# Two large groups' slices run in pairs, one scattering for both small groups, and a reordered front in an attention and mixture-of-experts kernel

## The chip, the cores and the metric

The kernel runs on one core of a Trainium2 chip. The metric is the device time in microseconds (us); less is better. The core's engines run side by side, each through its own queue in order: PE (TensorE) does matmuls and transposes and writes only to PSUM, DVE (VectorE) and ACT (ScalarE) do elementwise work and read PSUM, POOL (GpSimd) does elementwise work on SBUF, and SP issues DMA transfers.

## The reference

Three stages, in float32. First a linear attention, in four batches of 576 tokens, eight heads of 64:

```python
q_s = softmax(q, over the head dimension);  k_s = softmax(k, over the tokens)
kv  = einsum('bhsd,bhse->bhde', k_s, v)
x   = einsum('bhsd,bhde->bhse', q_s, kv)          # laid out as (2304, 512)
```

Then a mixture of experts: each token goes to the one of eight experts with the largest logit of `x @ w_gate`, up to a capacity of 576 tokens for each expert, and the output is `gate * (relu(x @ w1[e]) @ w2[e])`, with w1 512 x 1024 and w2 1024 x 512. The last stage is a second mixture with its own weights, added to its input, and only for tokens with `x @ w_skip > 0`.

## The kernel before

x lies transposed in SBUF: 128 partitions by 4 chunks of features by 576 tokens. A batch's attention is done in two halves of four heads: a and b are batch 0, c and d batch 1, e and f batch 2, g and i batch 3.

Nearly all tokens of a batch go to one expert. The kernel guesses that expert from the attention (`guess`), loads its weights, and runs all 576 tokens through it as a *large group*; the few tokens of another expert (at most 32) are gathered, put through it as a *small group* and scattered back. There are five large groups, in this order: first mixture for batches 0, 1 and 2, called (0, 0), (0, 1) and (0, 2), then second mixture for batches 0 and 1. Two small-group objects stand beside them: S (one small group, batch 2 of the first mixture) and T (two small groups, t = 0 and 1, batch 2 of the second mixture).

Each large group has 16 *slices*. Slices 0 to 7 make 128 features of the hidden layer each: 24 matmuls of 128x128 by 128x288 (`products`), because float32 is split into a high and a low part (`split`: ACT casts, DVE subtracts) and high-high, high-low and low-high are summed. `evacuate(s)` of these slices takes the result out of PSUM: ACT writes `hh` (relu, L876), then DVE writes `hl` (L877). Slices 8 to 15 make the output, two slices for each chunk, and the odd ones end with a DVE multiply by the gate into x. The slices use two PSUM pairs in turn (`banks`), so slice s can start once `evacuate(s-2)` has read its pair. `split_w(s)` makes a slice's weights `wh` (ACT) and `wl` (DVE) and runs two slices ahead; `L4` to `L7` are the loads of the group's later weights, `N0` to `N3` those of the next group's first, and `X0` to `X3` split the next group's x.

Between the slices stand the *words* of the table COURSE, one line for each slice, written by hand. Words left of the bar are issued between a slice's products and its evacuation, words right of it behind the evacuation. Since every engine goes through its queue in order, a line sets who stands behind whom. The words of an attention half (c.qm, c.km, ...): `qm` (DVE: maximum of q and its negative), `km`, `kt`, `kc` (maximum of k over the tokens: DVE, PE transposes with a DVE reduction, a PE matmul `pmax` and a DVE subtraction, L404), `ke` (ACT exponential of k, L411), `q1`, `q2`, `q3` (ACT: 7, 7 and 6 exponentials of q with sums, L334), `qn` (DVE normalization of q, L362 to L367), `kv` (PE and DVE), `qt` (PE transposes, ACT copies), `re` (PE, ACT copies into x). The words C1.g and C1.1 to C1.6 are the guess and the routing of batch 1; C1.5 is some 17 small DVE instructions, C1.6 some more with one ACT exponential between them. `G.0` and `G.3` make the gate.

Short PSUM results (`pl`, `pt`, `pmax`, `ptq`, `pts`, ...) share three banks in turn (`bank`, pool `pa` with `bufs=3`): the fourth waits until the first has been read.

The *front*, before group (0, 0), is straight code: a's and b's attention, with `warm_up(n)` putting n matmuls of no use in between. `first_products` runs slices 0 and 1 of the first group in halves of two chunks each, as chunks of x come ready.

A scattering (`put(t, i)`) of a small group multiplies the expert's output `y2` with a one-hot matrix `pT[t]` built by `places` and `place` (words v and a), in 8 matmuls (L1255), and adds the result to x in four DVE adds (L1259); i = 0, 1 stand for two chunks each.

Of the kernel before, what the change touches and what calls it, by code (L numbers as in the profile page):

```python
# [17 lines left out]
P = 128  # L18
# [22 lines left out]

COURSE = (
    ((0, 0), """
    L4 c.qm | C0.1 c.km
    c.q1 | c.kt
    L5 c.q2 | C0.2 c.kc
    C0.3 c.ke d.qm |
    L6 C0.4 c.q3 | c.kv  # L50
    C0.5 c.qn d.q1 |
    L7 d.km | c.qt d.kt
    C0.6 d.q2 | d.kc
    d.ke | c.re G.0
    d.q3 X0 | d.kv
    d.qn X1 e.ld |
    | d.qt
    | d.re C1.g N0
    X2 N1 | C1.1
    X3 N2 | C1.2  # L60
    C1.3 e.qm N3 f.ld | C1.4
    """),
    ((0, 1), """
    L4 C1.5 |
    e.km e.q1 | e.kt
    L5 C1.6 e.q2 | G.3 e.kc
    e.ke f.qm | G.1
    L6 e.q3 | e.kv
    e.qn f.q1 | G.2
    L7 f.km | e.qt f.kt  # L70
    f.q2 | f.kc
    f.ke | e.re
    f.q3 X0 | f.kv
    f.qn X1 |
    | f.qt
    | f.re C2.g N0
    X2 N1 | C2.1
    X3 N2 | C2.2
    C2.3 N3 g.ld | C2.4
    """),  # L80
    ((0, 2), """
    L4 C2.5 | M0.1
# [11 lines left out]
    N2 g.qn S.v0 | S.t03  # L94
    X2 | S.a0 g.qt
    N3 | S.t04
    X3 | S.u00 S.u01
    """),
    ((1, 0), """
    L4 G.3 | g.rw  # L100
    g.rx | M2.1
    L5 | M2.2 M1.1
    M2.3 | M2.4
# [14 lines left out]
    L4 G.3 | T.t03 O0.2  # L118
    | T.a0 i.rw
    L5 i.rx | T.t04 C3.1  # L120
    T.v1 | T.t10 T.u00
    L6 | T.u01 C3.2 G.1
    C3.3 | T.t11 C3.4 O0.3
    L7 C3.5 G.2 | T.t12 T.a1
    | T.t13
    Z B |
    | T.t14
    | T.u10
    | T.u11 O1.0
    | O2.0  # L130
    | O1.1 O2.1
    | O2.2
# [6 lines left out]
def kernel(  # L139
# [647 lines left out]
    class Group:  # L787
        def __init__(self, m, x, r, lo, last=False):
            self.m, self.x, self.r, self.lo, self.last = m, x, r, lo, last
            self.hs = []  # L790

        def load(self, i, half=None):
            if i < 4:
# [36 lines left out]
        early = []  # L830

        def products(self, s):
            if s < len(self.early):
                self.pt = self.early[s]
                return
            wh, wl = whs[s % NB], wls[s % NB]
            if s < NF:
                self.pt = banks()
                for a in range(2):
                    for c in range(NC):  # L840
                        for n, (u, w) in enumerate(((wh, xh), (wh, xl), (wl, xh))):
# [28 lines left out]

        def evacuate(self, s):
            if s < NF:
                hh = hp.tile([P, S], F32R, name="hh", tag="hh", bufs=NF)
                hl = hp.tile([P, S], F32R, name="hl", tag="hl", bufs=NF)
                src = self.pt[:, :, :HT]
# [11 lines left out]
            else:  # L887
                return
            y = halves(self.x[:, c])[:, w]
            src, gate = self.pt[:, w, :HT], halves(self.mg)[:, w]  # L890
# [37 lines left out]

        def gate(self):

            self.gate_weights()
# [18 lines left out]
    with tc.tile_pool(name="fp", bufs=1) as fp:  # L950
# [58 lines left out]
        def q_norm(h, hs):  # L1009
            h.inverse(hs)  # L1010
            h.norm(hs)

        def q_turn(h, c):
            pt = bank("ptq")
# [31 lines left out]
        warm_up(2)  # L1046
        k_sub(b)
        k_v(a)
        warm_up(16)
        v_ones(b)  # L1050
        k_exp(b)
        a.qm()
        a.exp_sub(H01, ALLJ)
        a.exps([(2, j) for j in range(NJ)])
        a.exp_act(H01, ALLJ)
        k_v(b)
        k_v_norm(a)
        b.qm()
        a.exps([(3, j) for j in range(NJ)])
        warm_up(12)  # L1060
        b.exp_sub(H01, ALLJ)
        k_v_norm(b)
        b.exps([(2, j) for j in range(NJ)])
        b.exp_act(H01, ALLJ)
        b.exps([(3, j) for j in range(NJ)])
        a.sum_bulk(H01, ALLJ)
        RT["C0"].guess()
        first.eid = load_reg(gid[0], [ET.SP], 7)
        first.load(0, 0)
# [43 lines left out]
    hp = ctx.enter_context(tc.tile_pool(name="hp", bufs=1, reuse_waits="tile"))  # L1113
# [8 lines left out]
    class Small:  # L1122
# [69 lines left out]
        def expert(self, t, step):  # L1192
# [4 lines left out]
            if step != 2:  # L1197
                for i in {0: (0, 1), 1: (2, 3), 3: (4, 5), 4: (6, 7)}[step]:
                    w = self.tw.pop(8 * t + i)
                    for g in range(4):  # L1200
                        if i < 4:
                            lhsT, rhs = self.xs[:, i, 32 * t:32 * t + 32], w[:, 256 * g:256 * g + 256]
                        else:
                            lhsT = self.hT[:, g % 2, 32 * (i - 4):32 * (i - 4) + 32]
                            rhs = w.rearrange("p (u d) -> p u d", u=2)[:, g % 2, 256 * (g // 2):256 * (g // 2) + 256]
                        nc.tensor.matmul(  # L1206
                            out=self.ph[32 * g:32 * g + 32, :256], lhsT=lhsT, rhs=rhs, start=(i % 4 == 0), stop=(i % 4 == 3)
                        )
                    self.load(8 * t + i + 3)
            if step == 1:  # L1210
# [7 lines left out]
                nc.vector.tensor_copy(out=self.hT, in_=pt[:, :2 * P].rearrange("p (u s) -> p u s", u=2))  # L1218
            elif step == 4:
                for i in range(2):  # L1220
                    sl, cs = slice(64 * i, 64 * i + 64), slice(2 * i, 2 * i + 2)
                    src = self.ph[sl, :256].rearrange("p (c d) -> p c d", c=2)
                    nc.scalar.copy(y2[0][sl, cs], src)
                    nc.vector.tensor_sub(y2[1][sl, cs], src, y2[0][sl, cs].bitcast(F32))

        def places(self, t):
            cs = hp.tile([P, TINY], F32, name="cs2", tag="cs2")
            nc.vector.tensor_scalar(out=cs, in0=iota, scalar1=self.r["tlo"][:, t:t + 1], scalar2=None, op0=ALU.add)
# [18 lines left out]
            nc.tensor.transpose(pt[:, 0:LAST], p4f[:LAST, 4], ident[:LAST, :LAST])  # L1247
            nc.scalar.copy(pT[:, 4 * P:S], pt[:, 0:LAST])

        def put(self, t, i):  # L1250
            for c in (2 * i, 2 * i + 1):
                for a in range(2):
                    pt = bank("pts")
                    for n, u in enumerate(y2):
                        nc.tensor.matmul(  # L1255
                            out=pt[:, :HT], lhsT=u[:, c], rhs=self.pT[t][:, tokens(a)], start=(n == 0), stop=(n == 1)
                        )
                    x = self.x[:, c, tokens(a)]
                    nc.vector.tensor_add(x, x, pt[:, :HT])  # L1259
# [83 lines left out]
    for kk, (_, plan) in enumerate(COURSE):  # L1343
        lines = plan.strip().split("\n")
        assert len(lines) == NS
        for i, line in enumerate(lines):
            before, _, after = line.partition("|")
            groups[kk].products(i)
            n = NS * kk + i + 2
            if n < NS * len(COURSE):  # L1350
                groups[n // NS].split_w(n % NS)
            for w in before.split():
                word(kk, w)
            if n < NS * len(COURSE) + 1:
# [16 lines left out]
    def all_groups(s):  # L1371
# [9 lines left out]
        with tc.If(n >= 1):  # L1381
            with tc.For_i(0, n, 1):
# [98 lines left out]
```

## Time and profile before

| | |
|---|---|
| median of 3 runs | 416.97 us (416.24 to 419.02) |
| the profiled execution | 416.55 us, of which the span of instructions 414.7 us |
| PE busy | 393.7 us, 95% of the span |
| DVE busy | 251.6 us, 61% |
| ACT busy | 182.3 us, 44% |
| POOL busy | 12.4 us, 3% |
| mean granted TensorE clock | 0.995 |

Busy times are of one profiled execution, and a busy PE isn't PE at its peak, as matmuls are pipelined. What an engine waits for is told by the profile's releasers. The group (0, 0) runs from about 45 to 113.8 us of the span, (0, 1) from 113.8 to 182.9 us.

### The profile page before, as it was taken

The numbers are of one execution on the slowest core, as the hardware profiler recorded it, in microseconds if no ns is written. First come the engines' busy times: TensorE is split into PE (matmuls) and PEld (weight loads), VectorE is DVE, ScalarE is ACT, GpSimd is POOL, SyncE is SP. The second block draws the span as 40 slices with busy tenths as digits, with TensorE's granted clock in tenths as the row PEclk, the third lists the DMA queues.
The fourth block names the chain that finished last, engine by engine and source line by source line (L and its number), as shares of the span: only waits on it lengthen the run. The fifth ranks groups of instructions, "written<-read, shape, count | busy, mean of one in ns | idle before, by whom it ended". The sixth has DMA issues, their size and how long they took to land.

```text
span 414.7 us, 8456 instructions
## 1 busy us (share of the span) xinstructions
PE 393.7 (95%) x3241; PEld 351.1 (85%) x3241; DVE 251.6 (61%) x640; ACT 182.3 (44%) x547; POOL 12.4 (3%) x46
## 2 busy tenths in 40 slices
PE   8989898999999999999999999999999999899892
PEld 4656797898999989799999888899998988799881
DVE  4874789463586846278546656367777736654432
ACT  1656675734357772324346622333375342331211
POOL 2400000000000000000000100000000000000000
PEclk9999999999999999999999999999999999999998
DMA  8829926100970400293355771116315556363133
GB/s 207 220 54 262 255 72 193 31 2 2 295 182 9 124 2 2 82 300 96 107 195 178 217 216 52 51 52 232 101 53 183 182 180 214 92 204 123 31 101 102
DMA packets 72535, 54.48 MB, mean 131 GB/s; under 512 B 18454, under 2 KB 67114, under 8 KB 72490
## 3 DMA queue, kind: packets, MB, share of 16 engines
q1 hardware_dynamic: 70536, 53.60, 44.4%
q10 hardware_dynamic: 1954, 0.31, 0.6%
q8 instruction: 26, 0.43, 0.4%
q14 instruction: 19, 0.16, 0.1%
HBM read 49.16 MB, written 4.73 MB: 130 GB/s over the span
## 4 chain that ended last, share of the span: by engine, by line
PE 85%; DVE 8%; ACT 3%; issue 2%; DVEq 0%; ACTq 0%
PE pair L863 31%; PE pair L842 25%; PE pair L535 3%; PE px L495 3%; PE pxs L1150 2%; PE pk L437 2%; PE pl L596 2%; PE pto L1284 2%; PE ph L1206 1%; PE py L1206 1%; PE pts L1255 1%; PE pk L992 1%; PE ptq L463 1%; DVE hl L877 1%; PE pair L822 1%
## 5 line engine op out<-in xcount | busy, mean ns | idle before, releaser
L863 PE MATMUL pair<-hh,wh 128*128 128x288 f32 x320 | 98.3, 307 | 0.0
L863 PE MATMUL pair<-hh,wl 128*128 128x288 f32 x320 | 94.6, 296 | 0.0
L863 PE MATMUL pair<-hl,wh 128*128 128x288 f32 x320 | 94.5, 295 | 0.0
L842 PE MATMUL pair<-xh,wh 128*128 128x288 f32 x304 | 92.8, 305 | 0.0
L842 PE MATMUL pair<-xl,wh 128*128 128x288 f32 x304 | 89.6, 295 | 0.0
L842 PE MATMUL pair<-xh,wl 128*128 128x288 f32 x304 | 89.5, 295 | 0.0
L785 DVE TENSOR_TENSOR wl<-ws,wh 128x512 fp32r<-128x512 f32 x80 | 54.9, 686 | 35.9 <-ACT wh L784 35.4
L863 PEld LDWEIGHTS pair<-hh,wh 128*128 128x128 f32 x320 | 60.5, 189 | 3.8 <-issue 2.6
L863 PEld LDWEIGHTS pair<-hl,wh 128*128 128x128 f32 x320 | 60.7, 190 | 0.1
L876 ACT ACTIVATE hh<-pair 128x576 fp32r<-128x576 f32 x40 | 25.8, 645 | 79.2 <-PE pair L842 77.4
L863 PEld LDWEIGHTS pair<-hh,wl 128*128 128x128 f32 x320 | 60.5, 189 | 0.0
L842 PEld LDWEIGHTS pair<-xh,wh 128*128 128x128 f32 x304 | 57.1, 188 | 2.2 <-issue 0.9
L842 PEld LDWEIGHTS pair<-xl,wh 128*128 128x128 f32 x304 | 57.2, 188 | 0.1
L842 PEld LDWEIGHTS pair<-xh,wl 128*128 128x128 f32 x304 | 57.1, 188 | 0.0
L877 DVE SCALAR_TENSOR_TENSOR hl<-pair,hh 128x576 fp32r<-128x576 f32 x40 | 30.2, 755 | 37.1 <-ACT hh L876 37.1
L784 ACT CAST wh<-ws 128x512 fp32r<-128x512 f32 x80 | 49.3, 620 | 2.2 <-DMA ws<-in_moe_w_dram 1.5
L334 ACT ACTIVATE eq<-qt,mx 128x64 f32<-128x64 f32 x140 | 46.7, 338 | 0.5 <-DVE mx L323 0.5
L334 ACT ACTIVATION_READ_ACCUMULATOR eq<-qt,mx 128x1 f32 x140 | 26.6, 190 | 0.0
L535 PE MATMUL pair<-warm 128*128 128x384 f16 x94 | 18.7, 346 | 1.6 <-DVE warm L952 1.6
L785 DVE TENSOR_TENSOR xl<-x,xh 128x576 fp32r<-128x576 f32 x20 | 14.9, 752 | 6.0 <-ACT xh L784 6.0
L1285 ACT COPY ot<-pto 128x256 f32<-128x256 f32 (+1 forms) x24 | 7.0, 315 | 26.0 <-PE pto L1284 26.0
L535 PEld LDWEIGHTS <-warm 128*128 128x128 f16 x94 | 9.3, 104 | 8.1 <-issue 2.1
(210 smaller groups left out, 500.2 us busy)
## 6 DMA issues: line engine op xcount, KB each, us to landing
ws<-in_moe_w_dram SPq DMA_DIRECT2D x39, 512.0 KB, 4.7
tw<-in_moe_w_dram SPq DMA_DIRECT2D x24, 512.0 KB, 4.6
kt<-in_k_dram SPq DMA_DIRECT2D x8, 512.0 KB, 7.5
qt<-in_q_dram SPq DMA_DIRECT2D x8, 512.0 KB, 6.5
out_dram<-ot SPq DMA_DIRECT2D x12, 256.0 KB, 2.7
vt<-in_v_dram SPq DMA_DIRECT2D x16, 128.0 KB, 4.8
vt<-in_v_dram SPq DMA_DIRECT2D x3, 512.0 KB
mg<-gate SPq DMA_DIRECT2D x4, 288.0 KB, 7.2
```

Of the source, the lines that this page charges most:

```text
L334: nc.scalar.activation(self.eqv[:, h, j], self.qt[:, h, j], AF.Exp, bias=self.mx[:, i:i + 1], accum_out=self.qz[:, i:i + 1])
L437: nc.tensor.matmul(out=pk[64 * g:64 * g + 64, c * D1 + o:c * D1 + o + n], lhsT=self.kt[:rows(j), 2 * c + g, j], rhs=ones32[:rows(j), 0:1] ...
L495: nc.tensor.matmul(out=pt, lhsT=self.kd[:, c], rhs=self.qT[:, c, 0:4 * P], start=True, stop=True)
L535: nc.tensor.matmul(out=pw[:, 0, :3 * P], lhsT=warm16[:, 0:P], rhs=warm16, start=True, stop=True)
L596: nc.tensor.matmul(out=pl[32 * c:32 * c + 32, :HT], lhsT=self.weights[:, c], rhs=self.chunk(c, tokens(a)), start=True, stop=True,)
L784: nc.scalar.copy(hi, src)
L785: nc.vector.tensor_tensor(out=lo, in0=src, in1=hi.bitcast(F32), op=ALU.subtract)
L842: nc.tensor.matmul(out=self.pt[:, a, :HT], lhsT=u[:, c], rhs=w[:, c, tokens(a)], start=(c == 0 and n == 0), stop=(c == NC - 1 and n == 2),)
L863: nc.tensor.matmul(out=self.pt[:, a, :HT], lhsT=p_[:, f], rhs=w[:, tokens(a)], start=(v == 0 and f == 0 and n == 0), stop=(v == 1 and f == ...
L876: nc.scalar.activation(halves(hh), src, AF.Relu)
L877: nc.vector.scalar_tensor_tensor(out=halves(hl), in0=src, scalar=0.0, in1=halves(hh).bitcast(F32), op0=ALU.max, op1=ALU.subtract,)
L1150: nc.tensor.matmul(out=self.px[:, c * self.w:(c + 1) * self.w], lhsT=self.xt[:rows(j), c * P:(c + 1) * P], rhs=self.pj[:rows(j), j], start ...
```

## The change

Four edits:

1. *Pairs.* A line of COURSE may be `=`: its slice has no words, and its evacuation is issued behind the next slice's products. Slices 0 to 11 of (0, 0) and of (0, 1) are put in six such pairs each, with the words of both lines behind the second one's products, and some words moved by a line or more (c.km and d.km, e.km, C1.g, N0 and N1, f.ld). Slices keep their results in `pts`, by number.
2. *Shared scattering.* For the second small group, the halves of `y2` are written to the other partitions, and `places` builds one matrix that holds both groups; `put(i)` scatters both at once. T's four scatterings become two, behind the last of its words t; S's two stay, the second in the next group's first line.
3. *Front.* The subtraction of the maximum from half of q goes from DVE (`exp_sub`) to POOL (`q_sub`), warm-ups are cut from 94 matmuls to 74, q's normalization is split between other steps, and both halves' way to x stands ahead of `first_products`, which now has no other work between its halves than splits.
4. `gate_weights` is no longer called in `gate`, but by the word G.3, or by its own call in the general code.

```diff
-    L4 c.qm | C0.1 c.km
-    c.q1 | c.kt
-    L5 c.q2 | C0.2 c.kc
-    C0.3 c.ke d.qm |
-    L6 C0.4 c.q3 | c.kv
-    C0.5 c.qn d.q1 |
-    L7 d.km | c.qt d.kt
-    C0.6 d.q2 | d.kc
-    d.ke | c.re G.0
-    d.q3 X0 | d.kv
-    d.qn X1 e.ld |
-    | d.qt
-    | d.re C1.g N0
-    X2 N1 | C1.1
-    X3 N2 | C1.2
-    C1.3 e.qm N3 f.ld | C1.4
+    =
+    L4 c.qm c.km | C0.1 c.q1 c.kt d.qm
+    =
+    L5 c.kc | c.ke C0.2 c.q2 c.q3 d.km
+    =
+    L6 C0.3 c.qn | c.kv d.kt d.q1 d.q2
+    =
+    L7 C0.4 d.kc | c.qt d.ke C0.5 C0.6 d.q3 G.3
+    =
+    G.0 d.qn | d.kv c.re e.ld
+    =
+    C1.g X0 N0 N1 | d.qt X1
+    N2 | d.re f.ld
+    X2 N3 | C1.1
+    X3 | C1.2
+    C1.3 e.qm e.km | C1.4
...
-    L4 C1.5 |
-    e.km e.q1 | e.kt
-    L5 C1.6 e.q2 | G.3 e.kc
-    e.ke f.qm | G.1
-    L6 e.q3 | e.kv
-    e.qn f.q1 | G.2
-    L7 f.km | e.qt f.kt
-    f.q2 | f.kc
-    f.ke | e.re
-    f.q3 X0 | f.kv
-    f.qn X1 |
-    | f.qt
-    | f.re C2.g N0
+    =
+    L4 C1.5 | C1.6 G.3 e.q1 e.kt
+    =
+    L5 e.kc | G.1 e.ke e.q2 e.q3 f.km
+    =
+    L6 f.qm e.qn | e.kv f.kt f.q1 f.q2
+    =
+    L7 G.2 f.kc | e.qt f.ke f.q3
+    =
+    f.qn | e.re f.kv
+    =
+    C2.g X0 N0 N1 | f.qt X1
+    N2 | f.re
...
-    X3 | S.u00 S.u01
+    X3 | S.u0
...
-    L4 G.3 | g.rw
+    L4 G.3 | S.u1 g.rw
...
-    T.v1 | T.t10 T.u00
-    L6 | T.u01 C3.2 G.1
+    T.v1 | T.t10
+    L6 | C3.2 G.1
...
-    | T.u10
-    | T.u11 O1.0
+    | T.u0
+    | T.u1 O1.0
...
+            self.run(s)
+            self.pts[s] = self.pt
+
+        def run(self, s):
...
+        def q_sub(h):
+            nc.gpsimd.tensor_tensor(
+                out=h.eqv[:, H01], in0=h.qt[:, H01], in1=h.spread_q(h.mx, H01, ALLJ), op=ALU.add
+            )
...
         a.qm()
-        a.exp_sub(H01, ALLJ)
+        q_sub(a)
+        warm_up(4)
+        k_v(b)
...
-        a.sum_bulk(H01, ALLJ)
+        q_norm(a, H01)
         RT["C0"].guess()
...
-        q_norm(a, H01)
-        q_norm(a, H23)
-        warm_up(8)
+        warm_up(2)
         a.turn_new()
         q_turn(a, 0)
-        warm_up(3)
+        q_norm(a, H23)
+        warm_up(4)
         q_turn(a, 1)
...
+        b.turn_new()
+        q_turn(b, 0)
         x_main(a, 1)
         x_last(a)
-        first.split_x(0)
-        first.split_x(1)
-        first.split_w(0)
         warm_up(2)
-        b.turn_new()
-        q_turn(b, 0)
-        warm_up(3)
         q_turn(b, 1)
         q_last(b)
-        first.first_products(0, range(0, 2))
-        first.split_w(1)
+        first.split_x(0)
         x_main(b, 0)
+        first.split_x(1)
+        warm_up(2)
         x_main(b, 1)
         x_last(b)
-        first.first_products(1, range(0, 2))
+        first.split_w(0)
+        warm_up(4)
+        first.first_products(0, range(0, 2))
         first.split_x(2)
         first.split_x(3)
+        first.split_w(1)
+        first.first_products(1, range(0, 2))
         first.first_products(0, range(2, 4))
         first.first_products(1, range(2, 4))
...
+                        o = 32 * (g ^ 2 if t and i >= 4 else g)
...
-                    in1=cs.unsqueeze(1).to_broadcast(bb),
+                    in1=cs[:, (g // 2) ^ t if self.n == 2 else 0].unsqueeze(1).to_broadcast(bb),
...
-        def put(self, t, i):
+        def put(self, i):
+            pT = self.pT[i if self.n == 2 else 0]
...
             groups[kk].products(i)
+            if i and lines[i - 1].strip() == "=":
+                groups[kk].evacuate(i - 1)
             n = NS * kk + i + 2
             if n < NS * len(COURSE):
                 groups[n // NS].split_w(n % NS)
+            if line.strip() == "=":
+                continue
```

## Rows read from the trace of the kernel before

**Rows 1.** Busy time by stage: stretch, its length, each engine's busy time (instructions), clock, DMA.

```profile
45.10:113.80 68.70, 65.17 (x565) 59.17 (x563) 43.42 (x111) 38.11 (x128) 1.46 (x6) 1.00 0.42 113
113.80:182.90 69.10, 67.65 (x565) 62.73 (x564) 43.02 (x105) 37.46 (x125) 1.17 (x4) 1.00 0.33 91
```

**Rows 2.** Timeline of the front: start, duration, engine, line, operation, count [idle before].

```profile
15.19 1.76 POOL L985 COPY va<-vt 128x256 f32<-128x256 f32 x5 [2.29 <-DMA vt<-in_v_dram]
...
19.36 2.98 PE L992 MATMUL pk<-va,kt 128*128 128x130 f32 x20
...
26.62 0.14 DVE L587 TENSOR_SCALAR gid<-gid 1x1 int32<-1x1 int32 x1
...
30.11 1.12 PE L495 MATMUL px<-qT,kvd 128*128 128x512 f32 x2
...
31.55 0.82 DVE L367 TENSOR_TENSOR eq<-eq,qz 128x640 f32<-128x640 f32 x1
...
44.95 0.29 PE L822 MATMUL pair<-xh,wl 128*128 128x288 f32 x1
...
47.06 0.39 PE L842 MATMUL pair<-xh,wh 128*128 128x288 f32 x1
```

**Rows 3.** Timeline of DVE in the second large group.

```profile
115.08 0.19 DVE L688 TENSOR_TENSOR keep<-pos,rem 128x40 f32<-128x40 f32 x1
...
117.98 0.76 DVE L877 SCALAR_TENSOR_TENSOR hl<-pair,hh 128x576 fp32r<-128x576 f32 x1 [0.26 <-ACT hh L876]
118.65 0.68 DVE L785 TENSOR_TENSOR wl<-ws,wh 128x512 fp32r<-128x512 f32 x1
119.25 0.69 DVE L378 TENSOR_TENSOR m<-kt 128x512 f32<-128x512 f32 x1
...
127.88 1.48 DVE L404 TENSOR_TENSOR kt<-kt,pmax 128x1280 f32<-128x1280 f32 x1
...
129.88 1.48 DVE L320 TENSOR_REDUCE mx<-qt 128x20 f32<-128x1280 f32 x1
...
137.15 1.49 DVE L367 TENSOR_TENSOR eq<-eq,qz 128x1280 f32<-128x1280 f32 x1
```

**Rows 4.** Timeline of PE in the first large group: a word's transposes.

```profile
71.13 0.41 PE L386 MATMUL pt<-c,m 128*128 128x128 f32 x2 [1.64 <-DVE m L380]
```

**Rows 5.** Timeline of ACT in the second large group: the exponential of k.

```profile
129.46 1.28 ACT L411 ACTIVATE kt<-kt 128x1280 f32<-128x1280 f32 x1 [2.22 <-DVE kt L404]
```

**Rows 6.** The chain that ended last, both large groups: start, us, what ran.

```profile
47.33 2.33 ACT eq L334 x14
...
121.06 0.41 PE pt L386 x2
...
145.78 3.18 PE pair L863 x24
```

**Rows 7.** The same chain at the scatterings of S (two pieces) and T.

```profile
250.16 3.39 PE pair L863 x24
...
256.79 3.18 PE pair L842 x24
...
347.99 0.99 PE pts L1255 x6
...
349.54 3.19 PE pair L842 x24
...
355.13 0.49 PE ptl L608 x4
```

**Rows 8.** Busy time by stage at the span's end, columns as in rows 1.

```profile
408.00:408.50 0.50, 0.49 (x3) 0.25 (x3) 0.00 (x0) 0.19 (x1) 0.00 (x0) 1.00 0.84 218
...
410.50:411.00 0.50, 0.00 (x0) 0.00 (x0) 0.00 (x0) 0.00 (x0) 0.00 (x0) 0.70 0.94 268
```

**Rows 9.** Busy time of the warm-up line alone at the start: PE, weight loads, clock, DMA.

```profile
1.55:4.75 3.20, 3.20 (x11) 1.59 (x12) 1.00 0.82 224
4.75:7.00 2.25, 2.25 (x16) 1.36 (x14) 1.00 1.19 275
```

More of the change, by code (lines that the diff above doesn't have):

```diff
@@ L45 @@
     ((0, 0), """
-    L4 c.qm | C0.1 c.km
-    c.q1 | c.kt
-    L5 c.q2 | C0.2 c.kc
-    C0.3 c.ke d.qm |
-    L6 C0.4 c.q3 | c.kv
-    C0.5 c.qn d.q1 |
-    L7 d.km | c.qt d.kt
-    C0.6 d.q2 | d.kc
-    d.ke | c.re G.0
-    d.q3 X0 | d.kv
-    d.qn X1 e.ld |
-    | d.qt
-    | d.re C1.g N0
-    X2 N1 | C1.1
-    X3 N2 | C1.2
-    C1.3 e.qm N3 f.ld | C1.4
+    =
[14 more added lines that the diff above has]
+    C1.3 e.qm e.km | C1.4
     """),
     ((0, 1), """
-    L4 C1.5 |
-    e.km e.q1 | e.kt
-    L5 C1.6 e.q2 | G.3 e.kc
-    e.ke f.qm | G.1
-    L6 e.q3 | e.kv
-    e.qn f.q1 | G.2
-    L7 f.km | e.qt f.kt
-    f.q2 | f.kc
-    f.ke | e.re
-    f.q3 X0 | f.kv
-    f.qn X1 |
-    | f.qt
-    | f.re C2.g N0
-    X2 N1 | C2.1
-    X3 N2 | C2.2
-    C2.3 N3 g.ld | C2.4
+    =
[11 more added lines that the diff above has]
+    N2 | f.re
+    X2 N3 | C2.1
+    X3 | C2.2
+    C2.3 g.ld | C2.4
     """),
@@ L790, in __init__ @@
             self.hs = []
+            self.pts = {}
         def load(self, i, half=None):
@@ L874, in evacuate @@
                 hl = hp.tile([P, S], F32R, name="hl", tag="hl", bufs=NF)
-                src = self.pt[:, :, :HT]
+                src = self.pts[s][:, :, :HT]
                 nc.scalar.activation(halves(hh), src, AF.Relu)
@@ L889, in evacuate @@
             y = halves(self.x[:, c])[:, w]
-            src, gate = self.pt[:, w, :HT], halves(self.mg)[:, w]
+            src, gate = self.pts[s][:, w, :HT], halves(self.mg)[:, w]
             if self.m == 0 and not self.general:
@@ L929, in gate @@
         def gate(self):
-            self.gate_weights()
             self.mg = hp.tile([P, S], F32, name="mg", tag="mg")
@@ L1007, in k_v_norm, with q_norm @@
                 nc.vector.tensor_mul(h.kd[sl, :, sl], pv[sl, :, g, 0:D], rz[sl].to_broadcast([64, 2, D]))
-        def q_norm(h, hs):
+        def q_norm(h, hs, eng=None):
             h.inverse(hs)
-            h.norm(hs)
+            (eng or nc.vector).tensor_tensor(
+                out=h.eqv[:, hs], in0=h.eqv[:, hs], in1=h.spread_q(h.qz, hs, ALLJ), op=ALU.mult
+            )
+        def q_sub(h):
+            nc.gpsimd.tensor_tensor(
+                out=h.eqv[:, H01], in0=h.qt[:, H01], in1=h.spread_q(h.mx, H01, ALLJ), op=ALU.add
+            )
         def q_turn(h, c):
@@ L1048 @@
         k_v(a)
-        warm_up(16)
         v_ones(b)
@@ L1052 @@
         a.qm()
-        a.exp_sub(H01, ALLJ)
+        q_sub(a)
+        warm_up(4)
+        k_v(b)
         a.exps([(2, j) for j in range(NJ)])
         a.exp_act(H01, ALLJ)
-        k_v(b)
         k_v_norm(a)
         b.qm()
+        q_sub(b)
         a.exps([(3, j) for j in range(NJ)])
-        warm_up(12)
-        b.exp_sub(H01, ALLJ)
+        a.sum_bulk(H01, ALLJ)
+        warm_up(6)
         k_v_norm(b)
@@ L1206, in expert @@
                         nc.tensor.matmul(
-                            out=self.ph[32 * g:32 * g + 32, :256], lhsT=lhsT, rhs=rhs, start=(i % 4 == 0), stop=(i % 4 == 3)
+                            out=self.ph[o:o + 32, :256], lhsT=lhsT, rhs=rhs, start=(i % 4 == 0), stop=(i % 4 == 3)
                         )
@@ L1220, in expert @@
                 for i in range(2):
-                    sl, cs = slice(64 * i, 64 * i + 64), slice(2 * i, 2 * i + 2)
+                    o = 64 * (i ^ t)
+                    sl, cs = slice(o, o + 64), slice(2 * i, 2 * i + 2)
                     src = self.ph[sl, :256].rearrange("p (c d) -> p c d", c=2)
@@ L1226, in places @@
         def places(self, t):
-            cs = hp.tile([P, TINY], F32, name="cs2", tag="cs2")
-            nc.vector.tensor_scalar(out=cs, in0=iota, scalar1=self.r["tlo"][:, t:t + 1], scalar2=None, op0=ALU.add)
+            cs = hp.tile([P, 2, TINY], F32, name="cs2", tag="cs2")
+            for u in range(self.n):
+                nc.vector.tensor_scalar(
+                    out=cs[:, u], in0=iota, scalar1=self.r["tlo"][:, u:u + 1], scalar2=None, op0=ALU.add
+                )
             self.p4 = hp.tile([P, NJ, 4, TINY], F32, name="p4", tag="ot", bufs=3)
@@ L1255, in put @@
                         nc.tensor.matmul(
-                            out=pt[:, :HT], lhsT=u[:, c], rhs=self.pT[t][:, tokens(a)], start=(n == 0), stop=(n == 1)
+                            out=pt[:, :HT], lhsT=u[:, c], rhs=pT[:, tokens(a)], start=(n == 0), stop=(n == 1)
                         )
@@ L1346 @@
         for i, line in enumerate(lines):
-            before, _, after = line.partition("|")
             groups[kk].products(i)
+            if i and lines[i - 1].strip() == "=":
+                groups[kk].evacuate(i - 1)
             n = NS * kk + i + 2
@@ L1351 @@
                 groups[n // NS].split_w(n % NS)
+            if line.strip() == "=":
+                continue
+            before, _, after = line.partition("|")
             for w in before.split():
@@ L1393, in all_groups @@
                     j.split_x(c, src)
+                j.gate_weights()
                 j.gate()
```

## The prediction

> **What bounds the kernel now.** I read the stages first. In the two large groups that change most, PE is busy 65.17 of 68.70 us and 67.65 of 69.10 us; DVE and ACT are at 54 to 63% [rows 1]. So PE sets the end, and an edit can win three things there: PE work that disappears, PE idle time (3.53 and 1.45 us in these groups) and the stretch before dense work begins. Next I read the chain that ended last: in the groups it is nearly all PE, broken where a transpose waits for DVE [rows 4, 6]. That says where a pair can lose: DVE and ACT go through their queues in order, and a slice can't start before the evacuation two slices back. Last I read the timeline of the front and the scatterings. The profiled execution (416.55 us) is 0.1% below the median of the runs, 416.97, so I sum against it; what lies around its span (1.85 us) stays.
>
> **Front.** The value product of b starts at 19.36 [rows 2] behind sixteen warm-ups. Now four stand there, and it can start at about 17.5: POOL's copies for it end at 16.95 [rows 2]. Its normalization and the guess follow, so the expert's number, ready at 26.76 before [rows 2], is ready at about 24.3, and all of SP's loads behind it move up by 2.4 us; SP isn't moved past anything. DVE then normalizes the rest of a and b, four pieces of about 1.2 us less one that now stands ahead of the guess, and one sum of 0.8: done at 28.7 instead of 31.55 + 0.82 = 32.37 [rows 2].
>
> That lead of 3.7 us isn't quite kept. PE has all of b's and the rest of a's transposes and products in one row (a pair of `px` matmuls takes about 1 us [rows 2]) and is through at about 33.3. Then come, in order, the copy of the last x, the casts and subtractions of chunks 2 and 3 and of slice 1's weights, with DVE free at about 37.1. Ten matmuls of slice 1's first half and 24 others, 0.133 us each (3.18 us for 24 [rows 6]), end at 41.6. Before, the last one starts at 44.95 [rows 2] and ends the stream at 45.08. I take P0 = 41.7, a lead of 3.4 us.
>
> POOL's subtraction, 640 elements with two inputs, doesn't occur in this trace. Its copies take 1.76 us for five times 256 elements [rows 2], or 0.88 us for 640: the lower end. Twice that, 1.76, for two inputs read one after the other, is the value I take; it starts at 17.05, when q's maximum is there and the copies are done, and ends 0.1 us after ACT asks for it. The upper end has no row; I keep 4 us, more than four times the copy. ACT has about 0.7 us of slack behind it, so 4 us would cost the front 1.5. A gain over the value taken can't come from it, since ACT is full there. The Trainium skill ("GPSIMD Engine Reference", Engine selection and its section 3.1) speaks against the move: the Vector engine is to do elementwise work, POOL being about twice as slow with two inputs, 4497 ns for 2048 elements; by that an estimate is 1.4 us for 640, and the sum would stay as it is.
>
> **Group (0, 0).** What the pairs leave alone is PE's work; what they save is a few changes between products and words: three fewer word blocks in each group, at 0.1 to 0.2 us (24 matmuls take 3.39 us behind a block of other matmuls and 3.18 otherwise [rows 7]). That is 0.3 to 0.6 us a group, and I take 0.3.
>
> At its first line the front's lead is paid back. Slice 0 ends at P0-1.6; `hh` follows at -1.4, `hl` at -0.7, and only then, in DVE's queue, `wl` (0.60), c.qm (1.60: the 1.48 of its reduction and a small instruction), c.km (1.81 until the transposes start: 119.25 to 121.06) [rows 3, 6]. So `pt` starts at P0+4.0, while PE was through with the router at P0+1.2: it waits 2.7 us. Slice 2 starts at P0+4.15 = 45.85; before, at 47.06 [rows 2]. The lead is 1.2 us.
>
> From there I walk the three queues line by line with the same spacings. PE waits 1.05 us before slice 7 (`hl` of slice 5 stands behind C0.3 and c.qn on DVE) and 0.85 us at c.qt, whose third transposed bank is the one `pmax` holds until `kc` has subtracted; elsewhere not. Together 4.6 us of idle time in place of 3.5. So of the 3.4 us, about 3.4 - 1.1 + 0.3 = 2.6 remain. The group ends at 113.8 - 2.6 = 111.2.
>
> **Group (0, 1).** Here I follow one chain, from the group's first matmul at 0. `hl` of slice 0 starts at 4.3 and takes 0.67; `wl` 0.60; C1.5, 2.64 (115.08 to the 0.26 us of idle time ahead of 117.98) [rows 3]; `hl` of slice 1, 0.67; the routing's exponential on ACT, 0.35: 9.2. Behind it on ACT, e.q1 takes 2.33 [rows 6] to 11.55; `wh` and `hh` of slice 2 to 12.6. DVE has finished `hl` and `wl` at 14.0, subtracts (1.48 [rows 3]) until 15.5. ACT's e.ke, e.q2 and e.q3 (1.28 [rows 5], then 4.33 for thirteen exponentials at the rate of e.q1) end at 21.1; `wh`, then `hh` of slice 4, `hl`, `wl`: 23.6; f.qm 1.60: 25.2; e.qn about 2.04 (1.49 plus two small ones [rows 3]): 27.2; `hl` of slice 5 0.76: 28.0. Slice 7 waits for this and ends at 31.25, `pmax` at 31.7. Meanwhile ACT's f.q1 and f.q2 start at 25.2 and put off `wh` of slice 8, and with it DVE's `kc`, to 33.85; e.qt needs that bank. Slice 8 starts at 34.4. Before, 145.78 - 113.8 = 32.0 [rows 1, 6]. The group loses 2.4 us: PE waits 0.55, 1.7 and 1.5 us in place of 1.45 in all.
>
> With 0.3 us for the changes the large groups end at 182.9 - 2.6 + 2.4 - 0.3 = 182.4, a gain of 0.5 us: the pairs eat the front. N0 and N1 stand a line earlier and f.ld ahead of N3 on SP, which puts N3 off by some 6 us; its weights are used a third of a group later, so I cost that at nothing (should that cover go, it is 6 us less what is left of some 12).
>
> **Scattering.** T.u00 costs PE 349.54 - 347.99 = 1.55 us; T.u01 from 352.73 to 355.13, 2.40 us, as its last matmuls wait for a bank that DVE frees late [rows 7]. Both vanish, 3.95 us; nothing else waits there, since the transposes behind them have their operand two lines earlier. The extra DVE instructions (one of 0.23 us in each of two words) hide beside slices. T's last two scatterings stay as they are. S loses: its two stand together before, 256.79 - 253.55 = 3.24 us [rows 7]; apart, the first pays 1.7 and the second, behind its line's `hl`, 2.4 as T.u01 did: 0.9 us more. Net gain 3.05 us.
>
> **The sum.** 416.55 - 0.5 - 3.05 = 413.0, which I predict.
>
> **Rivals.** *The pairs fit.* If ACT and DVE come out ahead where I have them late, PE has no waits: the front's 3.4, the idle 3.5 + 1.45, 0.6 for the changes and 3.05 come off: 404.5. For it: DVE and ACT are idle 40% of these groups [rows 1]. Against it: the chain in (0, 1) has hardly a gap. Half of it gives 408.5.
>
> *The clock falls in the new waits.* After the last matmuls (408.0 to 408.5) the granted clock is full until 410.5 and 0.70 in the next half microsecond [rows 8], so it drops towards 1.2 GHz about 2.2 us after PE stops. Waits of 2.7, 1.7 and 1.5 us are new. To climb back is dear: eleven warm-ups take 3.20 us at the start, and sixteen 2.25 later [rows 9] (0.29 and 0.14 us each, though the clock column prints 1.00 in both), so a fall loses some 1.6 us. One fall, in the 2.7 us, makes 414.6; three make 417.8, slower than before. It decides from a wait longer than those the trace shows without a fall, the longest 1.64 us [rows 4]. The page "TensorE: Matmul & The Clock Gate" of the Trainium skill (What's actually happening) has that rule: the default state is throttled, and activity releases it; by it the drop at the end is to be expected, and a drop at 2.7 us is possible.
>
> *POOL is slow.* From 5 us for a subtraction the front's whole lead is gone, and from about 6.5 us (four times what I take) the kernel is slower than before: at 8 us, 418. No row speaks for it.
>
> **How the numbers follow.** My forecast has 0.55, its own range 410.5 to 416 (each group's chain is good to about 1 us, the front to 0.7, POOL's upper end 1.5). The pairs fitting, wholly or half, 0.22; the clock falling 0.13; POOL 0.05; the rest, 0.05, spread. A range from 406.5 to 417.5 leaves out about a tenth below and less above. Repeats before lie within 0.7%, so 1% is what a measurement can tell from no change. Faster by over 1% means below 412.8: nearly half of my own case and all of the fitting pairs, 0.46. Over 421.1 only the ends of two rivals lie, 0.04. The rest, 0.50, is no change.
>
> **What would show it.** In the changed profile: the number `gid` near 24.4 us and the last first product near 41.6; a PE wait of 2 to 3 us for L380 at the first word transposes of (0, 0); waits of 1 us or more before slices 7 of both groups, released by `hl`; (0, 0) ending near 111 and (0, 1) near 182.4; from there to the span's end 228.8 us instead of 231.8, the scatterings' share. Wrong would be: both groups PE-bound throughout, a granted clock below 1 in a slice before the tail, or POOL's subtraction over 2.5 us.

## The result and the profile after

The changed kernel takes 413.36 us (median of 18 runs, 412.69 to 416.2), the kernel before 416.95 us (18 runs, 416.16 to 419.02): a ratio of 0.9912, 95% interval 0.9897 to 0.9928. That is 3.6 us less, or 0.9%, and 0.4 us from the forecast of 413.0. The profiled execution took 413.58 us, with a span of 411.8 us. Both spans are split here at the router's first matmul (`pl`) behind the front, the first matmul of (0, 1), the first matmul of (0, 2), and the end. These stand at 45.17, 113.80, 182.83 and 414.7 us before, and at 42.16, 112.55, 182.41 and 411.8 us after.

| | before | after | change | predicted |
|---|---|---|---|---|
| front, to the router's first matmul | 45.17 | 42.16 | -3.0 | -3.4 |
| the rest of (0, 0) | 68.63 | 70.39 | +1.8 | +0.8 |
| (0, 1) | 69.03 | 69.86 | +0.8 | +2.1 |
| from there to the span's end | 231.87 | 229.39 | -2.5 | -3.05 |

The sum is -2.9 us of span. The two terms of the groups are off by about 1 us and more, in opposite directions.

The two groups by stage, as in [rows 1]: windows of the changed kernel (the stretch, its length, busy time of PE, PE's loads, DVE, ACT and POOL, the granted clock, DMA share, GB/s).

```profile
42.10:112.60 70.50, 66.47 (x564) 60.40 (x563) 44.84 (x113) 38.08 (x127) 1.45 (x6) 0.98 0.52 134
112.60:182.50 69.90, 67.47 (x565) 62.56 (x564) 42.77 (x105) 37.52 (x125) 1.12 (x4) 1.00 0.30 90
```

PE is busier in the first (66.47 instead of 65.17 us) though it has no more work: the clock, 0.98, says why. In the second it idles 2.43 us instead of 1.45.

The front, as in [rows 2], from the timeline of the changed kernel:

```profile
14.33 2.98 PE L997 MATMUL pk<-x,x 128*128 128x130 f32 x20
...
17.84 1.25 POOL L1021 TENSOR_TENSOR eq<-qt,mx 128x640 f32<-128x640 f32 x1
17.90 1.36 PE L997 MATMUL pk<-va,kt 128*128 128x130 f32 x9
...
24.86 0.14 DVE L588 TENSOR_SCALAR gid<-gid 1x1 int32<-1x1 int32 x1
...
28.60 0.82 DVE L1016 TENSOR_TENSOR eq<-eq,qz 128x640 f32<-128x640 f32 x1
...
41.93 0.29 PE L824 MATMUL pair<-xh,wl 128*128 128x288 f32 x1
42.16 1.18 PE L597 MATMUL pl<-x,wg 128*32 128x288 f32 x16
```

The first and the last of these lines, in the kernel before:

```profile
13.84 2.98 PE L992 MATMUL pk<-x,x 128*128 128x130 f32 x20
...
45.17 1.18 PE L596 MATMUL pl<-x,wg 128*32 128x288 f32 x16
```

POOL's subtraction takes 1.25 us. The expert's number, the last normalization and the last first product stand 0.4 to 0.7 us behind the forecast; 0.5 us of that was lost ahead of the first changed step, in code that is the same in both kernels: the value product of a starts at 14.33 instead of 13.84 us. Counted from that product to the router, the front takes 27.83 us instead of 31.33. That is 3.5 us less, and the fairer measure of the lead, as the product's start differs between executions (13.84 to 15.30 us in the traces here).

PE in group (0, 0) and (0, 1), timeline (start, duration, the idle time ahead in brackets and what ended it):

```profile
46.11 0.42 PE L387 MATMUL pt<-c,m 128*128 128x128 f32 x2 [2.78 <-DVE m L381]
46.28 0.50 PE L848 MATMUL pair<-xh,wh 128*128 128x288 f32 x1
46.57 0.44 PE L848 MATMUL pair<-xl,wh 128*128 128x288 f32 x1
...
49.69 0.34 PE L848 MATMUL pair<-xh,wl 128*128 128x288 f32 x1
49.88 0.29 PE L848 MATMUL pair<-xh,wh 128*128 128x288 f32 x1
...
54.26 0.59 PE L399 MATMUL pmax<-dm,ones 128*128 128x256 f32 x2
...
68.24 0.40 PE L848 MATMUL pair<-xh,wh 128*128 128x288 f32 x1 [0.79 <-DVE hl L883]
...
73.18 1.09 PE L464 MATMUL ptq<-c,eq 128*128 128x128 f32 x8
...
135.54 0.40 PE L848 MATMUL pair<-xh,wh 128*128 128x288 f32 x1 [0.73 <-DVE hl L883]
...
140.33 0.40 PE L848 MATMUL pair<-xh,wh 128*128 128x288 f32 x1 [1.35 <-DVE hl L883]
...
144.40 1.10 PE L464 MATMUL ptq<-c,eq 128*128 128x128 f32 x8
144.95 1.48 DVE L405 TENSOR_TENSOR kt<-kt,pmax 128x1280 f32<-128x1280 f32 x1
```

The last line is DVE's, the others PE's. The wait of 2.78 us for c.km is where it was forecast. Behind it the matmuls of slice 2 start 0.24 us apart until 49.69, then 0.133 us apart. That is the clock's lower level, as the windows there say:

```profile
42.10:46.30 4.20, 1.42 (x20) 0.64 (x19) 4.04 (x8) 3.32 (x14) 0.00 (x0) 1.00 0.97 230
46.30:50.00 3.70, 3.70 (x18) 3.70 (x17) 3.29 (x6) 1.07 (x5) 0.00 (x0) 0.54 1.06 243
50.00:54.00 4.00, 4.00 (x33) 4.00 (x32) 1.36 (x2) 1.16 (x2) 0.00 (x0) 1.00 0.42 102
```

Granted 0.54 of full speed, so 1.2 GHz nearly throughout, then full again. The trap in reading this: a slow clock shows as a *busier* PE. The waits ahead of slices 6 and 7 are there with 0.7 to 1.35 us; the query transposes (L464) at 73.18 and 144.40 have no bracket, so the two bank waits of the forecast aren't there. The last four of those at 144.40 run although DVE reads `pmax` from 144.95 on.

The scatterings in the chain that ended last, as in [rows 7], of the changed kernel, and the two slices of the kernel before at which they are measured:

```profile
249.75 3.39 PE pair L869 x24
...
254.33 0.53 PE pts L1275 x2
...
259.94 0.53 PE pts L1275 x2
...
260.74 3.18 PE pair L848 x24
...
348.85 3.38 PE pair L848 x24
...
352.88 3.19 PE pair L848 x24
```

```profile
260.19 3.19 PE pair L842 x24
...
355.97 3.18 PE pair L842 x24
```

S: 260.74 - 249.75 = 10.99 us, before 260.19 - 250.16 = 10.03. T: 352.88 - 348.85 = 4.03, before 355.97 - 347.99 = 7.98. So T saves 3.95 us and S loses 0.96.

### The profile page after: what moved, and what is told of

Same layout as the page of the kernel before. It is cut to its first block, busy times and chain, and to the rows that moved or that the text cites. A ratio compares the mean times of both kernels' runs of the same rounds, so it can differ in the third digit from the quotient of the medians.

```text
span 411.8 us, 8370 instructions
## 1 busy us (share of the span) xinstructions
PE 389.0 (94%) x3205; PEld 348.0 (85%) x3205; DVE 246.7 (60%) x632; ACT 182.9 (44%) x547; POOL 14.7 (4%) x48
## 4 chain that ended last, share of the span: by engine, by line
PE 61%; DVE 3%; DMA 1%; ACT 1%; issue 0%; ACTq 0%; DVEq 0%
PE pair L869 25%; PE pair L848 19%; PE pxs L1163 2%; PE pto L1304 2%; PE ph L1221 1%; PE py L1221 1%; DMA tw<-in_moe_w_dram 1%; PE pk L438 1%; PE pl L597 1%; PE ptx L1178 1%; PE ptq L464 1%; PE px L496 1%; PE pts L1275 1%; PE ptl L609 1%; DVE hl L883 1%; ACT ot L1305 0%
## 5 line engine op out<-in xcount | busy, mean ns | idle before, releaser
L536 PE MATMUL pair<-warm 128*128 128x384 f16 x74 | 16.1, 359 | 1.6 <-DVE warm L957 1.6
L536 PEld LDWEIGHTS <-warm 128*128 128x128 f16 x74 | 7.5, 108 | 7.5 <-issue 3.2
```

The source lines that it names most:

```text
L536: nc.tensor.matmul(out=pw[:, 0, :3 * P], lhsT=warm16[:, 0:P], rhs=warm16, start=True, stop=True)
```

## The experiments

The theory behind the runs: the front gains 3 us, the shared scattering 2.5 to 3, and the pairs give back some 3, most of it through the 2.78 us wait and the clock behind it. The main rival was that the slices in pairs cost time by themselves (evacuations late in (0, 1), more contention), whatever stands at the first line.

**Parts of the change by themselves.** The kernel before with the shared scattering alone, and with scattering and front but the lines of before in (0, 0) and (0, 1):

```diff
 # the first: before, with put(i) and places of after; of the lines those of S and T, among them
-    X3 | S.u00 S.u01       -    T.v1 | T.t10 T.u00
+    X3 | S.u0              +    T.v1 | T.t10
 # the second: after, with all lines of (0, 0) and (0, 1) as before; in both kernels but
-    d.ke | c.re G.0
+    d.ke | c.re G.3 G.0
```

Of the first: 

> The kernel before with the shared scattering alone (S's second one in the next group's first line, as in the change); front and lines of the first two groups as before. My theory: T's two vanished scatterings take 3.95 us off PE, S's parting gives 0.9 back, so 413.9 us against 416.95 (ratio about 0.993). Rival, that what was taken from PE there is lost again behind it, for example to the loads of the small groups' weights: 416 to 417 us.

Of the second: 

> The changed kernel with the lines of the first two groups as before, so front and scattering without pairs. My theory: the pairs give the front's lead of some 3 us back (the wait of 2.8 us for the first word transposes of the first group, the fall of the granted clock in it, the waits before slices 6 and 7); without them the lead stays, as c.qm runs in DVE's idle time before slice 0 ends: 410.5 us, no granted clock below 1 before the tail. Rival, that pairs save something the other order doesn't have: 413.4 us or more.

Measured: 414.56 us, ratio 0.994 (0.9918 to 0.9961), and 411.92 us, ratio 0.9873 (0.985 to 0.9895). So without pairs the kernel is faster than the change as it stands, by 1.4 us. Both scatter (413.28 to 416.3; 410.46 to 412.64), and both medians lie above what was expected. In the first, five of seven runs have a mean granted clock of 0.995 to 0.997 and take 413.28 to 414.8 us; the two with 0.991 take 415.99 and 416.3. The traces show what can happen there. Windows, then PE's timeline, of the kernel with front and scattering:

```profile
66.00:70.00 4.00, 2.36 (x15) 2.16 (x15) 3.66 (x8) 1.81 (x5) 0.14 (x1) 0.78 0.83 207
70.00:74.00 4.00, 4.00 (x25) 3.95 (x25) 2.02 (x10) 2.95 (x16) 0.00 (x0) 0.79 0.34 78
74.00:78.00 4.00, 4.00 (x28) 3.52 (x27) 3.18 (x6) 2.04 (x3) 0.00 (x0) 1.00 0.01 2
```

```profile
68.56 0.66 PE L387 MATMUL pt<-c,m 128*128 128x128 f32 x2 [1.64 <-DVE m L381]
...
69.26 0.44 PE L848 MATMUL pair<-xl,wh 128*128 128x288 f32 x1
```

This is the same wait of 1.64 us, at the same word, that the kernel before has with the clock at 1.00 [rows 1, 4]; here the clock fell. The kernel with the scattering alone has it too, with the clock at 0.79 and 0.78 in the windows from 70 to 78 us of its profiled run, one of the two with 0.991. The prediction took 1.64 us as a length that the clock bears; it bears it sometimes. The repeats of the kernel before hint at the same: of 32 that were run beside the experiments, 28 have a mean clock of 0.995 to 0.997 and take 416.3 to 417.7 us, and four have 0.992 and take 418.7 to 419.0. Where the clock fell in those four isn't on record. In the kernel with front and scattering, four of the six runs have a mean granted clock of 0.990 to 0.992 and 411.7 to 412.64 us, the other two 0.995 and 0.996 and 410.46 and 410.79.

**The wait at the first line.** c.km's three maxima ahead of c.qm on DVE, everything else as changed; and the wait left as it is but filled:

```diff
-    L4 c.qm c.km | C0.1 c.q1 c.kt d.qm
+    L4 c.km c.qm | C0.1 c.q1 c.kt d.qm        # km_first
+    L4 c.qm c.km | C0.1 W c.q1 c.kt d.qm      # wait_filled; W: 16 matmuls on a constant
```

Of the first: 

> The changed kernel with c.km ahead of c.qm in the first pair, one swap of two words on DVE. My theory: the first word transposes wait 1.6 us less (1.2 instead of 2.8 us), and the granted clock doesn't fall, as the wait is under the longest that the kernel before showed without a fall (1.64 us): 3.1 us less than the changed kernel, 410.3 us. Rival, that ACT, whose first exponentials start 1.65 us later, is what sets the next slices: 412 us or more, with the wait moved to slice 4 or 6.

Of the second (the fillers compute nothing for the output): 

> The changed kernel with sixteen matmuls of no use (128 by 384, into a PSUM bank of their own) between the router and the first word transposes of the first group, so that PE isn't idle in its wait of 2.8 us; the wait itself stays. My theory: only the fall of the granted clock goes, 1.5 us less than the changed kernel, 411.9 us, and slices 2 and 3 run at 0.133 us a matmul throughout. Rival, that the clock falls for another reason, or that DVE's later waits take the gain: 413.4 us.

Measured: 410.36 us, ratio 0.9844 (0.9824 to 0.9863), and 411.84 us, ratio 0.9897 (0.9871 to 0.9924). Both as expected in the median: 3.0 us from one exchange of two words, half of it the clock. The interval of the second overlaps that of the change (0.9897 to 0.9928), and two of its six runs are slower, 412.68 us with a mean clock of 0.991 and 414.74 with 0.985, so the traces decide. In the trace of the first the wait is 1.18 us, and the clock holds:

```profile
45.11 0.41 PE L387 MATMUL pt<-c,m 128*128 128x128 f32 x2 [1.18 <-DVE m L381]
...
51.72 0.59 PE L399 MATMUL pmax<-dm,ones 128*128 128x256 f32 x2
```

From these transposes to `pmax` it takes 6.61 us; in the changed kernel, 54.26 - 46.11 = 8.15 us with the same work: the fall costs 1.54 us, close to the forecast's price of 1.6. In the second kernel the wait is full of matmuls, and the word transposes still stand 3.95 us behind the router's first matmul, as in the change:

```profile
41.93 1.18 PE L597 MATMUL pl<-x,wg 128*32 128x288 f32 x16
43.04 2.77 PE L1350 MATMUL pw<-c 128*128 128x384 f16 x16
45.88 0.41 PE L387 MATMUL pt<-c,m 128*128 128x128 f32 x2
...
52.49 0.59 PE L399 MATMUL pmax<-dm,ones 128*128 128x256 f32 x2
```

Here, too, it is 6.61 us to `pmax`, with the clock at 1.00. So PE was released no earlier, and the 1.54 us are gone because it did not idle. The exchange of the words gives 3.1 us of (0, 0) in the traces (67.26 instead of 70.39), 1.6 of the wait and 1.5 of the clock.

**The clock at the other wait.** The kernel with front and scattering, nine small matmuls in its 1.64 us wait:

```diff
-    L7 d.km | c.qt d.kt
+    L7 d.km | c.qt W d.kt
```

> The new front and the shared scattering, with both groups' lines as before (no pairs), and nine small matmuls on data that nothing reads, placed in PE's wait of 1.64 us for d's word transposes in group (0, 0). They compute nothing for the output. The kernel with this front but without the fillers took 411.92 us, and its trace shows the granted clock at 0.79 behind that wait, with eleven matmuls 0.24 us apart instead of 0.133: about 1.2 us. Clock theory (an idle PE of this length sometimes lets the clock fall, and this is why its runs spread from 410.46 to 412.64): about 410.6 in every run, granted clock 0.995 or more. Rival (the spread has another cause, such as DMA or DVE being late): no change, 411.9 with the same spread.

Measured: 410.84 us, ratio 0.9847 (0.9821 to 0.9872). Windows of this kernel:

```profile
66.00:70.00 4.00, 3.83 (x28) 3.00 (x29) 3.84 (x9) 1.85 (x5) 0.14 (x1) 1.00 0.84 219
70.00:74.00 4.00, 4.00 (x31) 3.95 (x30) 2.01 (x10) 3.32 (x17) 0.00 (x0) 1.00 0.36 83
```

PE isn't released a moment earlier (word transposes at 68.60 us), and the fall is gone: the rest of (0, 0) takes 68.66 us instead of 69.93. The median is 0.2 above the expected 410.6, the intervals of the two kernels overlap, and two of six runs still have a mean clock of 0.992 (411.58 and 411.6 us), which points to a fall elsewhere. With the clock out of the way this is also the measure of the pairs: the rest of (0, 0) is 68.66 us without them and 67.26 with them and c.km first. In (0, 0) pairs, with the words in that order, *gain* 1.4 us. The profiles say of what: PE idles 2.4 us in that stretch instead of 3.5 in the kernel before, and is busy for 64.83 us instead of 65.10.

**Pairs in (0, 0) alone.**

```diff
-    C1.3 e.qm e.km | C1.4
+    C1.3 e.qm | C1.4
...
-    =
-    L4 C1.5 | C1.6 G.3 e.q1 e.kt
+    L4 C1.5 |
+    e.km e.q1 | e.kt
...
```

> The changed kernel with c.km ahead of c.qm (410.36 us), its second group (0, 1) with the lines of before, so that only group (0, 0) has pairs. My theory: the pairs of (0, 1) cost what its two waits for hl show, 0.73 + 1.35 us, less the waits of before, 0.63 + 0.57, and less some changes between products and words: (0, 1) takes 69.9 us with pairs and 69.03 before, so the time falls by 0.9 to 409.5. The prediction's own chain would have it fall by 2.1 to 2.4, to 408.1. If pairs were worth something in (0, 1) it would be over 410.4.

Measured: 409.95 us, ratio 0.9829 (0.9804 to 0.9854). Beside the 410.36 that is 0.4 less, with intervals that overlap; the traces tell it apart: (0, 1) takes 69.04 us without pairs and 69.85 with them. So pairs lose 0.8 us there, as expected: PE idles 2.4 us with them and 1.5 without. Of the six runs, two have a mean clock of 0.989 (410.73 and 411.51 us), the others 0.994 and 409.65 to 409.96. In the profiled run the clock fell in the front, which the change thinned of warm-ups (windows); whether that is the reason isn't shown:

```profile
22.00:24.00 2.00, 1.54 (x13) 1.26 (x11) 1.85 (x6) 2.00 (x13) 1.37 (x6) 1.00 0.02 4
24.00:26.00 2.00, 1.73 (x14) 1.39 (x15) 1.32 (x10) 2.00 (x11) 0.00 (x0) 0.60 0.00 0
26.00:28.00 2.00, 2.00 (x10) 1.29 (x7) 1.90 (x4) 0.67 (x2) 0.00 (x0) 0.55 0.17 49
```

**S's two scatterings together again.**

```diff
-    X3 | S.u0          ...    L4 G.3 | S.u1 g.rw
+    X3 | S.u0 S.u1     ...    L4 G.3 | g.rw
```

> The changed kernel with c.km ahead of c.qm (410.36 us), both of S's scatterings behind the last line of (0, 2), as before; all else the same. My theory: apart, the second one waits 1.10 us for the x that DVE adds behind its line's hl; together the two cost 0.96 less: 409.4. Rival (the transposes that share a bank wait for DVE wherever they stand): no change, 410.4.

Measured: 409.9 us, ratio 0.9825 (0.9801 to 0.9849). In the chain of this kernel the two scatterings stand together, ending in ten matmuls in one row, and 256.84 - 246.82 = 10.02 us, 0.97 less; the intervals of the times overlap here as well:

```profile
246.82 3.39 PE pair L869 x24
...
251.41 2.03 PE pts L1275 x10
...
256.84 3.18 PE pair L848 x24
```

**The queries' normalization behind the evacuations.**

```diff
-    L6 C0.3 c.qn | c.kv d.kt ...     L6 f.qm e.qn | e.kv f.kt ...
+    L6 C0.3 | c.qn c.kv d.kt ...     L6 f.qm | e.qn e.kv f.kt ...
```

> The changed kernel with c.km ahead of c.qm (410.36 us), and in both groups the normalization of the first half's queries (c.qn, e.qn) moved on DVE from ahead of the two evacuations at its line to behind them. My theory: hl of slice 5 comes 2 us earlier, the waits of 0.79 us before slice 7 of (0, 0) and of 0.73 and 1.35 us before slices 6 and 7 of (0, 1) lose the 0.79 and the 1.35: 408.2, or 408.9 if the transposes of the queries then wait up to 0.35 us in each group. Rival (what comes late is ACT, with hh behind its exponentials, so hl can't come earlier): no change, 410.4.

Measured: 409.74 us, ratio 0.9819 (0.9793 to 0.9845). The first half of the theory holds: `hl` of slice 5 comes 1.9 us earlier, and the waits before slices 7 vanish. But new ones take their place at the query transposes, 0.35 us in (0, 0), as allowed for, and 1.15 in (0, 1):

```profile
142.32 0.66 PE L464 MATMUL ptq<-c,eq 128*128 128x128 f32 x4 [1.15 <-ACT qT L476]
```

The gain is 0.6 us in (0, 0) (66.6 instead of 67.26) and nothing in (0, 1) (69.84). The line also tells which bank the third of the transposed tiles takes: not `pmax`'s, which DVE reads until 143.9, but one freed by ACT's copy (L476) of the first transposed tile. So the three banks are not handed out in strict turn, as the description of the kernel has it; by what rule they are stays open.

**POOL's part.**

```diff
-            nc.gpsimd.tensor_tensor(out=h.eqv[:, H01], in0=h.qt[:, H01], ...)
+            nc.vector.tensor_tensor(out=h.eqv[:, H01], in0=h.qt[:, H01], ...)
```

> The changed kernel with c.km ahead of c.qm (410.36 us), the two subtractions of the front (640 elements by 128 partitions each) on DVE instead of POOL. POOL took 1.25 us for one; DVE takes 0.82 us for a like product. My theory: DVE is what makes the number of the expert late (it is busy for 6.5 of the 7.2 us from 17.1 to 24.3), so 1.64 us more on it puts that number, and P0 with it, off by 0.8 to 1.6: 411.2 to 412.0. Rival (ACT's exponentials set the front, and they get their operand 0.4 us earlier from DVE): 409.6 to 410.4.

(The profile of the kernel with c.km first has DVE busy for 6.10 us from 17.1 to 24.3, and ACT for 6.52; the 6.5 above is ACT's.) Measured: 411.77 us, ratio 0.9867 (0.9844 to 0.9889), 1.4 more than with POOL; no run is below 411.46, and with POOL none was above 411.03. DVE's timeline, then windows:

```profile
21.41 0.82 DVE L1021 TENSOR_TENSOR eq<-qt,mx 128x640 f32<-128x640 f32 x1
...
26.72 0.14 DVE L588 TENSOR_SCALAR gid<-gid 1x1 int32<-1x1 int32 x1
```

```profile
26.00:30.00 4.00, 3.56 (x17) 2.28 (x16) 3.69 (x12) 1.26 (x3) 0.00 (x0) 0.61 0.26 77
30.00:34.00 4.00, 4.00 (x10) 2.03 (x10) 1.22 (x4) 1.24 (x3) 0.00 (x0) 0.53 0.79 234
```

The expert's number comes 1.25 us later than with POOL (25.47 in the kernel with c.km first), with the clock at 1.00 from 22 to 26 us, and the five runs of 411.46 to 412.01 us lie by about as much above 410.36. So DVE sets that number, as the theory has it. The profiled run, 414.7 us, is the slowest of the six: behind two waits of PE for DVE, 1.43 and 0.90 us, the clock fell as well, and its router comes another 2.6 us late. All six have a lower mean clock (0.987 to 0.993) than the runs with POOL (0.995 to 0.996), so a part of the 1.4 us may be the clock's.

**What beats both.** Pairs in (0, 0) with c.km first and c.qn later, the lines of before in (0, 1), S together; and the same with four warm-ups in the front's wait ahead of the guess's last product:

```diff
+            if self.s == (0, 0):
+                warm_up(2)
+                warm_up(2)
             gx = self.tl([P, NC], "gx")
```

> What the runs so far say is better, together: pairs in group (0, 0) only, with c.km ahead of c.qm and c.qn behind the evacuations; the lines of before in (0, 1); S's scatterings together; the new front and T's shared scattering. Sum by the traces: 409.95 us (pairs in (0, 0) only) less 0.96 (S together) less 0.4 (c.qn later): 408.6. If the parts undo each other, 409.0 to 410.

> The kernel best with four more warm-up matmuls (on data that nothing reads) in the front's wait of 0.7 to 0.9 us ahead of the guess's last product. In one of the profiled runs the granted clock fell to 0.55 to 0.60 from 24 to 28 us, behind that wait. Clock theory: the runs with a mean granted clock of 0.989 to 0.990 (about one in five with this front) go away, the fastest stay: median 0.2 to 0.4 below best. Rival (the fall there comes from sparse work before it, not from this wait): no change.

Measured: 407.78 us (407.07 to 408.97), ratio 0.9777 (0.9751 to 0.9803), and 407.81 us (407.71 to 408.33), ratio 0.9776 (0.9754 to 0.9798). Both are 9.1 us below the kernel before. The parts add up: by stages the first takes 66.65 us in (0, 0), 69.04 in (0, 1) and 227.9 behind them, as the kernels with one of the parts each did (66.6, 69.04 and 228.4); the time is 0.8 less than the sum in the expectation. The warm-ups don't move the median, against the 0.2 to 0.4 us expected; no run with them has a mean clock below 0.996, while one of the five without has 0.991, which is too few to call shown.

## Why the prediction was right, and where it wasn't

- *Front: right.* The lead is 3.0 us instead of 3.4, and 3.5 counted from the value product of a. The value product of b starts at 17.90, the number is 1.8 us earlier, and, the 0.5 us of late start aside, the signs of the front stand within about 0.2 us of the forecast. The ten traces with this front and POOL's subtraction take 27.6 to 28.6 us from a's product to the router, the two with the old front 31.33 and 31.34. POOL's subtraction was sized at 1.76 and took 1.25; the Trainium skill's estimate of 1.4 ("GPSIMD Engine Reference", section 3.1) was nearer. Its advice to leave elementwise work to DVE (Engine selection) does not hold for this front: DVE had little room, and with the subtractions on it the median is 1.4 us higher.
- *The wait at the first line of (0, 0): right,* 2.78 us for 2.7, released by the word maxima behind c.qm.
- *The clock there: the rival came true.* It was given 0.13 and left out of the sum, and the fall costs 1.54 us. The sign that was named for being wrong, a granted clock below 1 in a slice before the tail, is in the trace. The fall is located in one profiled execution; the other 17 have mean clocks of 0.984 to 0.993 against 0.995 to 0.996 with c.km first, which agrees but does not tell where the clock fell (those with 0.993 are no faster than those with 0.989, and a mean takes in the end of the span, where PE is done). The step that failed is the price of nothing for this wait. The prediction had read that the clock drops some 2.2 us after PE stops, and forecast a wait of 2.7 us, longer than any that it had seen without a fall; so its own rows spoke for the fall more than a chance of 0.13 says. And "the longest 1.64 us", its mark of a harmless wait, was one outcome of something that goes either way. The Trainium skill's rule ("TensorE: Matmul & The Clock Gate", What's actually happening), that the throttled state is the default, agrees with the 0.54 behind this wait.
- *The bank waits at c.qt and e.qt (0.85 and 1.5 us): wrong.* They were worked out from a strict turn of the three banks, by which the third transposed tile waits for `pmax`'s reader. At 144.40 it doesn't wait, and where it does it waits for ACT. This is most of why (0, 1) lost 0.8 us instead of 2.1; the waits before slices 6 and 7, 0.55 and 1.7 by the forecast, are 0.73 and 1.35. In (0, 0) the wait before slice 7 is 0.79 for 1.05.
- *The pairs eat the front: right in the sum, not in the shape.* They give back 2.6 us of 3.0 (forecast 2.9 of 3.4), but by 3.1 us at one word, against a gain of 1.4 in the rest of (0, 0), and a loss of 0.8 in (0, 1). The rival that the pairs fit, PE without waits, did not occur: 2.4 us of idle time are left in each group even with c.km first.
- *Scattering: right.* T saves 3.95 us as said, S loses 0.96 for 0.9. The stretch behind (0, 1) is 2.5 us shorter in this profiled run instead of 3.05, but this differs between executions: in nine traces with this scattering it is 228.8 to 229.4 us, and in three of them (the scattering alone, and the two kernels with filled waits) 228.8, 3.0 less than before. In the trace of the change, PE's weight loads in T.t10 wait for the weights' DMA, which costs 0.3 us, and 0.2 us more pass between the last matmul and the end.

The total came out within 0.4 us by luck. In (0, 0) the change of +1.8 us is 0.5 of idle time (4.0 us for 3.5; forecast 4.6) and 1.54 of the clock, less 0.3 for fewer changes between products and words, as forecast. In (0, 1) the +0.8 us is 1.0 of idle time (2.4 us for 1.45; forecast 3.75) less 0.15 for the changes. So a fall of the clock that was left out and 1.9 us of idle time that did not occur nearly cancel.

## What to carry to other kernels

A wait of PE has two prices, its length and what the clock does behind it: read the granted clock and the spacing of the matmuls right behind the wait, over several executions, before calling it harmless. Where words are gathered in one place, the order within the line decides: put first on DVE what PE waits for. And sum a change by stages between fixed points of PE's queue, the first of them ahead of what was changed: a total that is right to 0.1% hid errors of 1.5 and 1.9 us.

## What the runs showed of the hardware

The same 1.64 us of idle PE, behind the same work, left the granted clock at 1.00 in the profiled run of the kernel before and at 0.78 to 0.79 in those of two kernels with the same lines; so the length of a wait alone does not settle it. After 1.18 us none of the six traces that have it shows a fall at that place. After 2.78 us it came in the one trace that has it, and with the wait filled by matmuls it did not. A fall with some eleven slow matmuls cost 1.3 us of the group (69.93 and 69.94 instead of 68.66 and 68.63), one with fourteen 1.5. POOL's subtraction of 128x640 elements took 1.25 us beside DVE's 0.82 to 0.95.
